# Router decisions worked out in the PSUM bank of the last logits, one bank of logits per head pair, and a slot list cast three units later

## The chip, the cores and the metric

The kernel runs on one core of one Trainium2 chip. Its engines are TensorE (PE, matmuls; PEld is its weight load), VectorE (DVE), ScalarE (ACT), GpSimd (POOL) and SyncE (SP, which issues most of the DMAs). Each takes its instructions from a queue of its own, in order, and waits at an instruction until the semaphores it needs are set. The metric is the device time of one execution in microseconds (us).

## What is computed

Clustered attention feeds a routed mixture of experts.

```python
# attention: q, k, v of (4, 8, 768, 64), centroids (8, 16, 64)
q_assign = argmax(einsum('bhsd,hcd->bhsc', q_n, c_n)); k_assign = ...   # normalized
mask = q_assign[:, :, :, None] == k_assign[:, :, None, :]
scores = where(mask, scale * q @ k.T, -1e9)
x = softmax(scores) @ v             # -> (3072, 512): 4 batches x 768 tokens, 8 heads x 64

# router: 4 groups x 4 experts, F = 1024
g_logits = x @ w_group              # top group, its softmax weight g_w
e_logits = xg @ w_expert[g]         # top expert in the group, its weight e_w
h = maximum(xg[mask_e] @ w1[g, e], 0.0)
out[tok] = (g_w * e_w)[:, None] * (h @ w2[g, e])
```

Both softmax weights come down to 1/sum(exp(l - max l)), since the chosen logit is the greatest.

## The kernel before

**Attention.** There are 32 heads (4 batches of 8). The work of a head is cut into 9 units, 288 in all; in the loop over units, TensorE does for each one `fine` (4 matmuls of scores into a psf bank, L346 and L347), one pass of coarse scores for a later head (psc, L304, from which VectorE takes row maxima, L307) and the product with V of an earlier unit (`av`, 16 matmuls, L372 and L373, into pso). ScalarE takes the exponential (L351, p), GpSimd its low half (L353, pl). Numbers are kept in pairs of fp16 or bf16 (a high and a low half) so that matmuls are fast and nearly exact.

**Beside the units.** Everything else of the attention phase is dealt out between units: normalizing and assigning the next heads (L201 and others), row maxima of a head turned by a transpose (L328, with the copy mr L331, which goes by DMA into a row of A that `fine` needs), and the router. Steps that need a bank of the pool psm (2 banks) give `yield PSM, delay, priority` and are queued in `turns`; `beside` lets one of them in per unit (`GAP` = 1). A plain `yield` waits one unit. The program written in this way is then ordered per engine by a scheduler with a time model of its own, so that an instruction may stand a little before or after where it was written.

**The router, per batch.** `finish` writes a head's result as two halves into the tile xs. After the last head of a batch `store` sends xs to xbuf in HBM, whose rows are the tokens. After every second head `logits` transposes the pair's 128 columns (L596), copies them (L599, xTr), multiplies by the router's weights (L604) and adds the result to lg in SBUF (L610), twice, for token tiles 0 to 2 and 3 to 5. After a batch's last pair `decide` works on 30 groups of 4 logits for each of 128 partitions (6 token tiles x 5 groups): the maximum (rmx L628), the first place that has it (req L630 and L631, rmw L633, roh L635), exp of the differences and its sums (L638 to L641), the one-hot expert of each token (roe L643), the weight (L645 to L650, pay). Rank matmuls over roe (L655 to L659) give each token its place among those of its expert; L662 to L667 make the row number rdi, and six scatters on GpSimd (L678) write token number and weight into the table in HBM.

**The first expert, beside the last batch.** After the third batch `first` picks the expert with most tokens (L803 to L809, f0i), loads its weights (st, L760) and splits them (L780 to L788). Once the third batch's scatters are out it loads that expert's slots from the table (tabA, L836), waits `FIRST + 1` units, casts the slot list (idA, L842) and gathers those rows of xbuf (L916). Its first products are done on TensorE beside the last batch's decision (psh, L954).

**After the last batch** a sorted list of experts is made, the table is read back (tb, L1103), a small matmul by a permutation (L1133) picks slot lists, and then the remaining experts run, each with loads (st), splits (L767, L770), gathers and products (L954, L976, L990).

## Time and profile before

| | us |
|---|---|
| time, median of 3 runs (lowest, highest) | 770.17 (769.25, 773.49) |
| the profiled execution | 771.85 |
| its span | 770.0 |
| TensorE busy | 728.0 (95% of the span) |
| VectorE, GpSimd, ScalarE busy | 604.4, 493.2, 465.8 |

The profiled execution is 1.85 us longer than its span (what lies around it), and 1.68 us above the median. Busy time is the sum over an engine's instructions, without waits. A wait is charged to the engine that stood idle and to the instruction that released it.

### The profile page before, as it was taken

Reading aid. Unit: us, or ns where it says so; the run is one execution under the profiler, and the core shown is the slowest. Engines: PE = TensorE matmul, PEld = TensorE weight load, DVE = VectorE, ACT = ScalarE, POOL = GpSimd, SP = SyncE. Lnnn points to the kernel's source line nnn. Section 1 sums busy time; section 2 is a strip of 40 time slices with the busy share of each in tenths; the row PEclk is TensorE's granted clock in tenths of the full one; section 3 lists DMA queues with packets and bytes.
Section 4 is the critical chain, followed back from the end, with each engine's and each line's share of the span. In section 5 each row is a group of like instructions: output and inputs, shape, how many; then the busy total and the mean of one; then the engine's idle time right before and its main releaser. Section 6 shows DMA issues by size and latency. Waiting matters only on the chain. (4 is left out here: it accounts for less than half of the span.)

```text
span 770.0 us, 26718 instructions
## 1 busy us (share of the span) xinstructions
PE 728.0 (95%) x11086; PEld 625.0 (81%) x11086; DVE 604.4 (78%) x1209; ACT 465.8 (60%) x910; POOL 493.2 (64%) x522
## 2 busy tenths in 40 slices
PE   5899999999999999997999889999999999999996
PEld 3677788878888788886878666788779999999996
DVE  5998978899788998988875545867598898888861
ACT  4567877768777687675886236435444455555542
POOL 9568687779977799776982433425545455654432
PEclk7799999999999999999999999999999999999998
DMA  8857534435345452223321397866778788888821
GB/s 247 198 149 176 147 90 119 156 95 148 88 118 159 95 149 59 68 95 111 84 57 49 65 316 252 261 201 211 228 245 249 236 270 267 260 279 278 267 74 49
DMA packets 80392, 128.28 MB, mean 167 GB/s; under 512 B 8851, under 2 KB 47251, under 8 KB 80264
## 3 DMA queue, kind: packets, MB, share of 16 engines
q1 hardware_dynamic: 74492, 113.12, 50.0%
q0 software_dynamic: 5616, 13.35, 5.1%
q8 instruction: 88, 1.44, 0.9%
q14 instruction: 40, 0.33, 0.1%
q10 hardware_dynamic: 156, 0.03, 0.0%
HBM read 93.20 MB, written 14.11 MB: 139 GB/s over the span
## 5 line engine op out<-in xcount | busy, mean ns | idle before, releaser
L353 POOL TENSOR_TENSOR pl<-p 128x512 f16<-128x512 f32 x278 | 286.8, 1050 | 81.6 <-ACT p L351 77.0
L307 DVE TENSOR_REDUCE mpart<-psc 128x1 f32<-128x512 f32 (+1 forms) x282 | 189.6, 682 | 32.8 <-PE psc L304 32.8
L351 ACT ACTIVATE p<-psf 128x512 f32<-128x512 f32 x288 | 168.5, 595 | 53.2 <-PE psf L347 46.1
L372 PE MATMUL pso<-V,p 128*128 128x65 f16 x1152 | 161.6, 193 | 0.0
L372 PE MATMUL pso<-V,pl 128*128 128x65 f16 x1152 | 161.2, 194 | 0.0
L373 PE MATMUL pso<-V,pl 128*128 128x64 f16 x1152 | 161.0, 191 | 0.0
L373 PE MATMUL pso<-V,p 128*128 128x64 f16 x1152 | 160.9, 191 | 0.0
L346 PE MATMUL psf<-A 82*128 82x384 f16 (+2 forms) x576 | 143.3, 274 | 4.8 <-ACT p L351 3.1
L347 PE MATMUL psf<-B 128*128 128x384 f16 (+2 forms) x576 | 143.6, 274 | 0.0
L373 PEld LDWEIGHTS <-p 128*128 128x128 bf16 x1152 | 112.6, 98 | 21.3 <-issue 0.2
L372 PEld LDWEIGHTS <-p 128*128 128x128 bf16 x1152 | 112.1, 97 | 9.2 <-issue 1.4
L373 PEld LDWEIGHTS <-pl 128*128 128x128 f16 x1152 | 112.8, 98 | 0.7 <-issue 0.4
L304 PE MATMUL psc<-A 80*128 80x512 f16 (+1 forms) x376 | 108.8, 331 | 4.3 <-DVE mpart L307 3.3
L372 PEld LDWEIGHTS <-pl 128*128 128x128 f16 x1152 | 111.2, 97 | 0.3
L957 DVE SCALAR_TENSOR_TENSOR hl<-psh,hh 128x160 f16<-128x160 f32 (+14 forms) x136 | 50.1, 370 | 66.9 <-ACT hh L956 55.7
L956 ACT ACTIVATE hh<-psh 128x160 f16<-128x160 f32 (+14 forms) x136 | 46.1, 346 | 66.8 <-PE psh L954 64.1
L954 PE MATMUL psh<-xT,wh0a 128*128 128x288 f16 (+7 forms) x512 | 74.7, 255 | 0.0
L916 POOL DMA_INDIRECT xg<-xbuf,ri x32 | 41.4, 1294 | 42.4 <-PE psm L926 21.1
L347 PEld LDWEIGHTS <-B 128*128 128x128 f16 x576 | 56.6, 98 | 14.3 <-issue 5.6
L954 PE MATMUL psh<-xT,wh0b 128*128 128x272 f16 (+6 forms) x448 | 65.2, 254 | 2.1 <-DVE xT L928 1.1
L954 PE MATMUL psh<-xT,wl0a 128*128 128x288 f16 (+7 forms) x256 | 64.0, 255 | 0.0
L346 PEld LDWEIGHTS <-A 82*128 82x128 f16 x576 | 55.5, 98 | 10.3 <-DMA A<-mr 1.0
(311 smaller groups left out, 1744.7 us busy)
## 6 DMA issues: line engine op xcount, KB each, us to landing
st<-w SPq DMA_DIRECT2D x128, 512.0 KB
B<-parts SPq DMA_DIRECT2D x64, 192.0 KB
kx<-kT SPq DMA_DIRECT2D x16, 384.0 KB
qx<-qT SPq DMA_DIRECT2D x16, 384.0 KB
vx<-vr SPq DMA_DIRECT2D x16, 384.0 KB
A<-parts SPq DMA_DIRECT2D x32, 192.0 KB
xbuf<-xs SPq DMA_DIRECT2D x4, 1536.0 KB
A<-mk SPq DMA_DIRECT2D x56, 24.0 KB
```

What stands on the lines that cost most here:

```text
L304: last["mm"] = nc.tensor.matmul(out=pc[:, off:off + k1 - k0], lhsT=QA[h % 8][0:80, c * P:(c + 1) * P], rhs=KA[h % 8][0:80, k0:k1], start=T ...
L307: nc.vector.tensor_reduce(out=(mp[:, 0, 0:1], mp[:, :, 1], mp[:, 1, 0:1])[i], in_=pc.rearrange("p (a x) -> p a x", a=n), axis=AX.X, op=ALU ...
L346: nc.tensor.matmul(out=o, lhsT=KA[h % 8][0:82, ks], rhs=QA[h % 8][0:82, q0:q1], start=True, stop=False)
L347: nc.tensor.matmul(out=o, lhsT=KBs[h][:, ks], rhs=QBs[h][:, q0:q1], start=False, stop=True)
L351: cfg["exp"] = nc.scalar.activation(out=p32, in_=pf, func=AF.Exp, scale=QK / (SQ * SQ))
L353: lo = (nc.vector if u in (EARLY if h < 2 else DVE_LO[h % 8] if h < NH - 2 else DVE_END) else nc.gpsimd).tensor_tensor(out=pl, in0=p32, in ...
L372: nc.tensor.matmul(out=O[:, col:col + 65], lhsT=p[:, bs], rhs=vh, start=c == 0 and q == 0 and i == 0, stop=False, skip_group_check=True)
L373: nc.tensor.matmul(out=O[:, col:col + 64], lhsT=p[:, bs], rhs=vl, start=False, stop=c == NCH - 1 and i == 1, skip_group_check=True)
L916: self.got = nc.gpsimd.indirect_dma_start(out=xg[0:n].rearrange("p a d -> p (a d)"), out_offset=None, in_offset=bass.IndirectOffsetOnAxis( ...
L954: self.mm = nc.tensor.matmul(out=ph[:, 0:M], lhsT=w[:, k, fs], rhs=xT[:, a, k], start=i == 0, stop=i == 3 * KD - 1)
L956: nc.scalar.activation(out=hh[:, f], in_=ph[:, 0:M], func=AF.Relu)
L957: self.ev = nc.vector.scalar_tensor_tensor(out=hl[:, f], in0=ph[:, 0:M], scalar=0.0, in1=hh[:, f], op0=ALU.max, op1=ALU.subtract)
```

## The change

The tile xs gets the head pair as its outermost axis, so that a pair is one contiguous block; each pair is stored to xbuf as soon as it is there (16 stores of 384 KB instead of 4 of 1536 KB, in pieces of 512 bytes instead of 2 KB). `logits` does both transposes first, then 18 matmuls into one psm bank and one add of 120 elements per partition instead of two of 60: three turns per pair instead of four. The last pair's sum stays in its PSUM bank, and `decide` works in four stretches of that bank: the logits, req, roh and rdf of before. Its values are fp32 now instead of fp16. The one-hot roe is made before the exponential's branch, for which one copy is added (rog: the group one-hot in SBUF). The bank is held until the weighted sum rss. The first plain `yield` of `decide` moves behind rss, and `first` waits `FIRST + 4` units for the cast.

```diff
-            if hh == H - 1:
-                R.store(b, XSt[b])
             if hh % 2 == 1:
+                R.store(b, XSt[b], hh // 2)
                 gens = [R.logits(b, XSt[b], hh // 2, [(ps_m, "psm"), (ps_f, "psf")] if last else None)]
...
-        for i in range(2):
+        xT = self.sm.tile([P, T, 2, P], F16, name="xTr")
+        banks = banks or [(self.psm, "psm")] * 2
+        for i, (pool, nm) in enumerate(banks):
             yield PSM, 0, 1
...
-            xT = self.sm.tile([P, n, 2, P], F16, name="xTr", bufs=2)
-            self.last["a"] = nc.scalar.copy(out=xT, in_=tp)
-            yield PSM, 1, 1
-            lp = pool.tile([P, 512], F32, name=nm)[:, 0:n * 20].rearrange("p (c x) -> p c x", x=20)
...
+            self.last["a"] = nc.scalar.copy(out=xT[:, n * i:n * i + n], in_=tp)
+        yield PSM, 1, 1
+        bank = self.psm.tile([P, 512], F32, name="psm")
+        lp = bank[:, 0:T * 20].rearrange("p (c x) -> p c x", x=20)
...
+        else:
+            nc.vector.tensor_tensor(out=lp, in0=lp, in1=lg, op=ALU.add)
+            self.lg[b] = bank
...
-        lv = lg.rearrange("p t (g x) -> p (t g) x", x=4)
+        lv, eq, oh, df = (self.lg[b][:, n * G * 4:(n + 1) * G * 4].rearrange("p (g x) -> p g x", x=4) for n in range(4))
...
+        nc.vector.tensor_tensor(out=oh, in0=eq, in1=mw.broadcast_to([P, G, 4]), op=ALU.is_equal)
+        oh = oh.rearrange("p (t g) x -> p t g x", g=5)
+        oe = sm.tile([P, T, 4, 4], F16, name="roe")
+        og = sm.tile([P, T, 4], F32, name="rog")
+        nc.vector.tensor_copy(out=og, in_=oh[:, :, 0])
+        nc.vector.tensor_tensor(out=oe, in0=oh[:, :, 1:5], in1=og.broadcast_to([P, T, 4, 4]), op=ALU.mult)
         nc.vector.tensor_tensor(out=df, in0=lv, in1=mx.broadcast_to([P, G, 4]), op=ALU.subtract)
...
         nc.vector.tensor_tensor(out=ss, in0=se[:, :, 1:5], in1=oh[:, :, 0], op=ALU.mult)
+        yield
...
-        for _ in range(FIRST + 1):
+        for _ in range(FIRST + 4):
             yield
```

On VectorE, from the add of the first batch's last logits to its one-hot experts (before: lg and req, roh, rmw, rmx; L307 are row maxima of the units between):

```order
L610 TENSOR_TENSOR lg<-psm,lg 128x60
L628 TENSOR_REDUCE rmx<-lg 128x30
L630 TENSOR_TENSOR req<-lg,rmx 128x120
L307 TENSOR_REDUCE mpart_198<-psc 128x2
L631 TENSOR_TENSOR req<-req,desc_502 128x120
L638 TENSOR_TENSOR rdf<-lg,rmx 128x120
L633 TENSOR_REDUCE rmw<-req 128x30
L635 TENSOR_TENSOR roh<-req,rmw 128x120
L307 TENSOR_REDUCE mpart_198<-psc 128x1
L641 TENSOR_REDUCE rse<-rdf 128x30
L643 TENSOR_TENSOR roe<-roh 128x96
```

and with the change (psm is the bank that holds all four stretches):

```order
L612 TENSOR_TENSOR psm<-psm,lg 128x120
L630 TENSOR_REDUCE rmx<-psm 128x30
L307 TENSOR_REDUCE mpart_200<-psc 128x1
L631 TENSOR_TENSOR psm<-psm,rmx 128x120
L313 TENSOR_REDUCE m_3880<-mpart_200 128x6
L632 TENSOR_TENSOR psm<-psm,desc_502 128x120
L307 TENSOR_REDUCE mpart_198<-psc 128x1
L634 TENSOR_REDUCE rmw<-psm 128x30
L635 TENSOR_TENSOR psm<-psm,rmw 128x120
L307 TENSOR_REDUCE mpart_198<-psc 128x2
L639 COPY rog<-psm 128x24
L640 TENSOR_TENSOR roe<-psm,rog 128x96
```

The exponential's two steps (L638 and L641 of before) have gone behind roe; one L307 and an L313 more, and the copy rog, stand before it.

On TensorE the rank matmuls of the same batch stood at the end of an `av` (before):

```order
L372 MATMUL pso<-V_173,pl 128x65
L373 LDWEIGHTS pl
L373 MATMUL pso<-V_173,pl 128x64
L655 LDWEIGHTS low
L655 MATMUL psm<-roe,low 128x96
```

and stand now after its first matmul, behind the `fine` and the psc of that unit:

```order
L347 MATMUL psf<-B 128x384
L304 LDWEIGHTS A_169
L304 MATMUL psc<-A_169 128x512
L372 LDWEIGHTS p_3734
L372 MATMUL pso<-V_173,p_3734 128x65
L657 LDWEIGHTS low
L657 MATMUL psm<-roe,low 128x96
```

Three units of TensorE lie between the last logits and the rank in both, and one `fine` and one psc more with the change.

On VectorE, after the last batch's rank matmuls, the row numbers (rdi) came after the weights (pay) before; with the change the weights (L644 to L652) are last, between the first comparisons of the slot list (st, L1100):

```order
L664 TENSOR_TENSOR rps<-psm,cb 128x96
L665 TENSOR_TENSOR rps<-rps,roe 128x96
L644 TENSOR_REDUCE rse<-psm 128x30
L667 TENSOR_REDUCE rds<-rps 128x6
L646 TENSOR_TENSOR rss<-rse,psm 128x24
L669 CAST rdi<-rds 128x6
L670 TENSOR_TENSOR cb<-psm,cb 128x16
L649 TENSOR_REDUCE res<-rss 128x6
L1100 TENSOR_SCALAR st<-sl,rds 128x128
L650 TENSOR_SCALAR res<-res 128x6
L1060 TENSOR_TENSOR c_11365<-cb,ebase 128x16
L1100 TENSOR_SCALAR st<-sl,rds 128x128
```

Four rows behind this piece, with one more comparison (L1100) among them, stands L652, which writes pay; the scatters need both pay and rdi. TensorE's up-projection matmuls (L954 before) between the last logits and the last rank are 20 before and 27 with the change. From L1133 on, TensorE, VectorE, ScalarE and GpSimd have the same instructions in the same order in both.

## Rows read from the trace of the kernel before

**Rows 1.** Busy time by stretch: the stretch (us), its length, then for each engine the busy us and, in brackets, the instructions; at the end TensorE's granted clock as a share of full speed, the DMA engines' busy share and GB/s.

```profile
100.00:200.00 100.00, 98.03 (x1909) 82.06 (x1906) 86.69 (x193) 75.47 (x148) 81.90 (x80) 1.00 0.43 118
300.00:400.00 100.00, 93.94 (x1804) 78.39 (x1802) 85.03 (x193) 72.40 (x141) 81.66 (x81) 1.00 0.30 87
490.00:600.00 110.00, 110.00 (x994) 91.60 (x992) 84.46 (x127) 49.99 (x94) 51.36 (x44) 1.00 0.75 238
452.00:455.00 3.00, 3.00 (x14) 1.93 (x13) 2.06 (x2) 0.29 (x1) 2.50 (x2) 0.50 0.99 313
```

**Rows 2.** Waits between 20 and 425 us, by the engine and line that waited and by the engine and line waited for: us in total, times, longest us.

```profile
PE psm L655 <- DVE roe L643: 4.1, 3, 1.4
...
PE psc L304 <- DVE mpart L307: 3.3, 7, 0.8
...
PE psf L346 <- ACT p L351: 3.1, 5, 1.5
...
DVE idA L842 <- DMA tabA<-table: 1.9, 2, 1.2
...
ACT wh L780 <- DMA st<-w: 1.5, 1, 1.5
```

**Rows 3.** TensorE (PE) in order of time, at places between 152 and 393 us: start us, us, engine, line, operation, out<-in, count, and in square brackets the idle time just before it with what ended that.

```profile
152.20 0.37 PE L604 MATMUL psm<-WR,xTr 128*128 128x20 f16 x9
152.42 0.27 PE L346 MATMUL psf<-A 82*128 82x256 f16 x1
...
153.09 0.19 PE L372 MATMUL pso<-V,p 128*128 128x65 f16 x1
...
153.58 0.22 PE L346 MATMUL psf<-A 82*128 82x128 f16 x1
...
157.46 0.20 PE L655 MATMUL psm<-roe,low 128*128 128x96 f16 x1 [1.36 <-DVE roe L643]
...
164.47 0.38 PE L304 MATMUL psc<-A 80*128 80x512 f16 x1 [0.19 <-DVE mpart L307]
...
260.29 0.38 PE L304 MATMUL psc<-A 80*128 80x512 f16 x1 [0.20 <-DVE mpart L307]
...
354.13 0.27 PE L304 MATMUL psc<-A 80*128 80x256 f16 x1 [0.74 <-DVE mpart L307]
...
358.47 0.27 PE L304 MATMUL psc<-A 80*128 80x256 f16 x1 [0.69 <-DVE mpart L307]
...
392.57 0.33 PE L596 MATMUL psm<-ident,xs 128*128 128x128 f16 x3 [0.91 <-DVE lg L610]
```

**Rows 4.** VectorE (DVE) in order of time around the decision of the first batch, 152 to 159 us; same columns.

```profile
152.61 0.22 DVE L610 TENSOR_TENSOR lg<-psm,lg 128x60 f32<-128x60 f32 x1
152.86 0.28 DVE L628 TENSOR_REDUCE rmx<-lg 128x30 f32<-128x120 f32 x1
153.18 0.86 DVE L630 TENSOR_TENSOR req<-lg,rmx 128x120 f16<-128x120 f32 x1
153.95 0.68 DVE L307 TENSOR_REDUCE mpart<-psc 128x2 f32<-128x512 f32 x1
...
155.43 0.82 DVE L635 TENSOR_TENSOR roh<-req,rmw 128x120 f16<-128x120 f16 x1
...
156.95 0.45 DVE L643 TENSOR_TENSOR roe<-roh 128x96 f16<-128x96 f16 x1
```

**Rows 5.** All instructions of a line, four lines on VectorE: count, shortest/median/longest ns, first and last start, shapes.

```profile
L630 DVE TENSOR_TENSOR req<-lg,rmx x4: 284/854/856, 153.2 to 423.7; 128x120 f16<-128x120 f32 x4
...
L631 DVE TENSOR_TENSOR req<-req,desc x4: 216/450/452, 154.6 to 424.1; 128x120 f16<-128x120 f16 x4
...
L662 DVE TENSOR_TENSOR rps<-psm,cb x4: 249/250/251, 158.5 to 426.2; 128x96 f32<-128x96 f32 x4
...
L201 DVE TENSOR_TENSOR parts<-psm,parts x48: 540/548/559, 62.6 to 321.6; 128x384 f16<-128x384 f32 x48
```

**Rows 6.** VectorE around the decision of the last batch, 423 to 427.3 us, in order of time.

```profile
423.13 0.21 DVE L610 TENSOR_TENSOR lg<-psf,lg 128x60 f32<-128x60 f32 x1
...
425.04 0.26 DVE L643 TENSOR_TENSOR roe<-roh 128x96 f16<-128x96 f16 x1
...
426.16 0.25 DVE L662 TENSOR_TENSOR rps<-psm,cb 128x96 f32<-128x96 f32 x1
...
427.06 0.17 DVE L667 CAST rdi<-rds 128x6 int32<-128x6 f32 x1
```

**Rows 7.** TensorE in the same stretch.

```profile
422.36 0.38 PE L604 MATMUL psf<-WR,xTr 128*128 128x20 f16 x9
422.59 0.28 PE L954 MATMUL psh<-xTA,wl 128*128 128x288 f16 x1
...
424.99 0.29 PE L954 MATMUL psh<-xTA,wh 128*128 128x288 f16 x1
425.35 0.20 PE L655 MATMUL psm<-roe,low 128*128 128x96 f16 x1
```

**Rows 8.** GpSimd (POOL) in order of time, its first scatter of the last batch, and under it two pieces of the chain that ended last (start us, us, what).

```profile
427.51 1.02 POOL L678 DMA_INDIRECT table<-pay,rdi  x1 [9.34 <-DVE st L1098]
...
434.10 8.07 DMA table<-pay,rdi
...
449.49 1.58 PE psm L1133 x12
```

73 lines of the change are left out of this document (32 added, 41 removed).

## Prediction

> **What bounds the kernel now.** I read the stretches first, then the waits, then TensorE, VectorE and GpSimd in order of time where a router step stands. In the attention phase TensorE is busy 98.03 of 100 us, and in the expert phase for every one of 110 us; the third batch's stretch, in which the first expert is prepared, has 93.94 of 100 [rows 1]. So the end is set by TensorE nearly everywhere, and an edit counts for the time that TensorE stands idle because of it, plus what it adds to the one stretch after the last batch in which TensorE has too little to do. In the waits the reader is to see how little the router holds TensorE up: 4.1 us in three waits of the rank matmul for roe, 3.3 us in seven waits of psc for VectorE's row maxima, 3.1 us in five for p [rows 2].
>
> The three rank waits are 1.36, 1.36 and 1.35 us, one per batch but the last (4.1 in all, 1.4 the longest, with the first one shown) [rows 2, 3]. VectorE causes them: from the add of the last logits at 152.61 to the end of roe at 156.95 + 0.45 = 157.40 are 4.79 us, and TensorE starts the rank at 157.46 [rows 3, 4]. Two of the steps in it are the dear ones, req (0.86) and roh (0.82) [rows 4]. The last batch's req takes 0.284 where the others take 0.854, at the same shape [rows 5]; there GpSimd has nothing to do (9.34 us idle up to its first scatter) [rows 8]. Steps that read PSUM show no such spread: 0.249 to 0.251 over four times, 0.540 to 0.559 over 48 [rows 5].
>
> The last batch has another path. Add at 423.13, roe at 425.04, rank 425.35, rps 426.16, rdi 427.06, first scatter 427.51 [rows 6 to 8]. The six scatters, the transfer of the last (8.07 us from 434.10) and the reading back follow one after the other to the matmul at 449.49 [rows 8], where the expert phase begins and from where TensorE is full. What the first scatter is late, the end is late.
>
> **The change, part by part.**
>
> *Decision in PSUM, three batches.* Price of a step of 120 elements on PSUM in fp32: 0.250 for 96 and 0.548 for 384 elements [rows 5] give (0.548 - 0.250) / 288 = 1.03 ns an element, so 0.275 for 120. Below it cannot be much under the 0.250 row; above, 0.548 is the end, if the fixed part counts for more. I take 0.275, from the nearest row, and 0.32 from start to start in a dependent chain, as 152.86 to 153.18 is for a 0.28 step [rows 4]. The stretch from the add to roe has eight router steps: six of 0.32 (1.92), rog of 24 elements at 0.20 (an estimate, between nothing and the 0.32) and roe itself, 0.28. Between them stand three L307, each 0.61 of VectorE's queue (an estimate: the 0.68 of the row at 153.95 less the overlap with the next, by which req's 0.86 takes 0.77 to that row), 1.83, and an L313 of 0.10 (an estimate, half of rog's): 4.33 us instead of 4.79. So the chain itself is only 0.46 shorter, since one L307 and rog come into it. The larger gain is in TensorE's order. A unit is 153.58 - 152.42 = 1.16 us [rows 3], and the rank stands a `fine` and a psc later, 153.09 - 152.42 = 0.67 [rows 3] (bounds: nothing, if that work was ahead of the rank's place in time anyway, and 0.67). New wait: 1.36 - 0.46 - 0.67 = 0.23; with an L307 that itself comes up to 0.2 late for its psc I take 0.40. Gain 0.95 per batch, 2.9 for three. Bounds: 4.1 (no wait left) and, at 0.548 a step, a loss (rival C). The psc waits of 0.19 and 0.20 after the first two batches [rows 3] are VectorE's arrears of the same work; they go: 0.4.
>
> Here the Trainium skill bears on both sides. The trace shows 0.854 against 0.284 for the same step of two SBUF operands, with and without GpSimd at work [rows 5, 8]. "SBUF — State Buffer", section "Who interferes with whom", says that a VectorE instruction with two SBUF inputs contends with a GpSimd instruction that reads SBUF, and that the one that comes second is blocked; by it all steps moved to PSUM are freed, and the trace agrees. Against the change stands "VectorE: DVE Perf Modes", section "Rules for kernel authors": with PSUM sources accept the slow mode, or copy to SBUF first where many operations follow. By that rule alone the step req x desc (0.216 in the clear, 0.450 beside GpSimd [rows 5]) would be better off in SBUF by 0.06 in the last batch and worse by 0.18 in the others; no term of the sum depends on it.
>
> *The bank that is held.* psm has two banks, and `decide` now holds one until rss. The rank takes the other; the next transpose of row maxima (L328, one unit behind the rank on TensorE) takes the held one. It arrives after the rank (at least the 0.20 of its first row), the rest of an `av` (153.58 - 153.09 = 0.49) and a `fine` and psc (0.67) [rows 3]: some 1.4 us behind the rank's start. rss needs by then the subtraction (0.32), the exponential on ScalarE (0.25 to 0.86, the ends of [rows 5], for no row here shows one), and the sum, rps and rss (0.8), with an L307 (0.61) beside the exponential: 1.7 to 2.0 behind roe, and the rank starts when roe ends. So up to 0.6 a batch, and nothing where the exponential runs beside L307 and TensorE itself comes late to L328 (it has just waited for roe); I take 0.13 a batch, near the lower end, 0.4 in all, with 1.8 as the other end.
>
> *Third batch.* Its waits of 0.74 and 0.69 for psc, 1.5 for st and 0.91 behind the cast idA [rows 2, 3] come from the first expert's own steps. The routing is done earlier, f0i and the splits move with it, and so does the last scatter; the cast, written three units later behind it, stands 16 units behind that scatter in both orders (counted by L353 on GpSimd and L307 on VectorE). I leave them as they are: 0, with 2.5 (all VectorE's share gone) and -1 as ends.
>
> *Stores, layout, logits.* Twelve more store DMAs go through SP's queue, between loads that are due much later; DMA engines are busy 0.43 and 0.30 of those stretches [rows 1]. Transposes and matmuls are as many as before. Each pair saves one VectorE add; VectorE has idle time there (86.69 of 100 busy [rows 1]). 0; if the cover were gone, a store of 384 KB in front of a load would cost 1.4 us once (118 GB/s at a busy share of 0.43 is 274 GB/s [rows 1]), less than the one of 1536 KB.
>
> *The last batch.* Both halves' transposes first, so the 18 matmuls stand together: the second half's 9 take 422.59 - 422.36 = 0.23 [rows 7], and all 18 end at 422.36 + 0.46 = 422.82. Then 27 up-projection matmuls instead of 20, each (424.99 - 422.59) / 19 = 0.126 [rows 7]: 3.41, so TensorE reaches the rank at 426.23. VectorE, with the add at 423.2, six steps of 0.32, rog, roe and an hl between them (0.4, an estimate between the 0.25 and 0.55 of [rows 5]), has roe at 426.0: covered. The rank is 0.88 later than 425.35 [rows 7]. rps follows by 0.81 as before (425.35 to 426.16) [rows 6, 7]: 427.04. From rps to pay are now 15 steps in two interleaved chains. In the same kind of interleaving rps to rdi took 427.06 - 426.16 = 0.90 for seven steps [rows 6], 0.13 a step and more where a step depends on the one before; I take 0.14 x 15 = 2.1, so pay starts at 429.14, and the scatter 0.45 after it (427.06 to 427.51) [rows 6, 8], at 429.6: 2.1 later. Bounds: 0.9 (only the rank counts, if pay were in time) and 3.2. I take 2.0. GpSimd's scatters are a chain, so all of it reaches the end. From L1133 on the order is the same, a plain shift.
>
> *Sum:* -2.9 - 0.4 + 0.4 + 0 + 2.0 = -0.9 us on the profiled 771.85, 770.95; on the median of 770.17 it is 769.3. I give the time in terms of the median.
>
> **Rivals.**
>
> A, *the attention gain is larger*. VectorE's freed time also takes the psc waits of the third batch (0.74 + 0.69), the wait of 0.91 and that for st (TensorE's share 1.5) [rows 2, 3], and the rank waits go whole (4.1): -4.1 - 0.4 - 3.8 + 2.0 = -6.3, 763.9. For it: each of these ends at VectorE. Against: L804 and L812's kind of step stays in SBUF, and GpSimd stays full there (81.66 of 100 [rows 1]). 0.20.
>
> B, *gain and loss cancel through the bank*: L328 waits 0.5 to 0.8 for rss in each batch, which gives back 2 us instead of 0.4: 770.9. For it: the pool has two banks only. Against: rss stands 0.3 to 0.6 us behind L328's arrival only if everything falls together. 0.16.
>
> C, *slower: a PSUM step costs its fixed 0.55*. Place: the eight steps before roe. Price: 0.23 a step x 8 = 1.8; the rank waits become 0.4 + 1.8 = 2.2 instead of 1.36, +2.5 for three, and the last batch has 1.6 more ahead of its rank and 1 behind: +2.5 + 0.4 + 2.0 + 2.6 = +7.5, 777.7. It decides from about 0.30 a step on, where the 0.9 of the sum is used up. Against it: the 0.250 row of 96 elements [rows 5]. 0.07.
>
> E, *slower: the last batch alone*. pay comes 1 us later than summed (each of its steps waits for the one before and the slot list's steps stand between), and TensorE's longer idle time before 449.49 prolongs the stretch at half clock (0.50 from 452 to 455 [rows 1]) by as much as 1.5 us: 771.8. Against: TensorE's order to there is filled with the first expert's products. 0.11.
>
> D, *the change doesn't do what it says*: the cast still waits for tabA as before (two waits, 1.9 us [rows 2]). It is part of my sum; that it does go gives 0.9 us less, 768.4.
>
> **How the numbers follow.** Forecast 0.46, A 0.20, B 0.16, C 0.07, E 0.11; D changes the size of the forecast and has no chance of its own. The forecast's own range is 767.5 to 771.5. To hold 8 in 10 it goes down most of the way to A, 764.8, and up past B and E, 773.2. A measurement of this kernel tells apart about 0.5%, 3.85 us: faster than 766.3 is A's greater part, 0.18; slower than 774.0 is C and a part of E, 0.11; between, 0.71.
>
> **What would show it.** Rank waits for roe under 0.6 us each, with the comparison steps at 0.26 to 0.30 in all four batches; L328 with a wait for rss of at most 0.5; the cast idA still waiting over 1 us for tabA; the last batch's first scatter 2 us after 427.51 in its own time, with pay the later of its two inputs; TensorE full from L1133 on. Wrong: PSUM steps over 0.35, rank waits of 1 us or more, or psc waits that are gone in the third batch.

## The result, and the profile of the changed kernel

The changed kernel takes 774.55 us (median of 16 runs, 771.88 to 779.86) where the kernel before takes 770.37 on the same chip (16 runs, 767.31 to 773.49). The ratio is 1.0072, with an interval of 1.0057 to 1.0088: slower by 0.7%. The forecast of 769.3 had the wrong sign, and the time lies above the range's upper end of 773.2. The profiled execution of the changed kernel takes 778.18 us, with a span of 776.1, and lies 3.6 above its median; that of the kernel before takes 771.85, with a span of 770.0, and lies 1.5 above. So the profiles are read for where time goes, and the ratios for how much.

First two of the stretches of [rows 1] in the changed kernel, and three shorter ones: two around the first expert's preparation and one ahead of the expert phase.

```profile
100.00:200.00 100.00, 99.24 (x1936) 83.33 (x1933) 86.36 (x192) 76.20 (x150) 82.87 (x82) 1.00 0.43 118
300.00:400.00 100.00, 91.28 (x1674) 75.27 (x1673) 79.07 (x182) 66.24 (x128) 76.49 (x76) 0.95 0.32 85
...
345.00:360.00 15.00, 10.19 (x187) 8.10 (x184) 10.30 (x34) 5.13 (x11) 8.21 (x8) 1.00 0.44 103
360.00:368.00 8.00, 6.91 (x75) 5.25 (x75) 4.93 (x10) 5.64 (x13) 5.83 (x6) 0.57 0.53 191
...
456.00:460.00 4.00, 1.79 (x9) 1.79 (x9) 1.96 (x4) 2.56 (x5) 0.00 (x0) 0.50 0.90 311
```

Two of the kernel before, for the places that have no row ahead of the prediction:

```profile
345.00:360.00 15.00, 12.16 (x220) 9.65 (x217) 14.58 (x42) 6.24 (x14) 10.35 (x11) 1.00 0.09 24
360.00:368.00 8.00, 6.46 (x120) 5.37 (x118) 5.37 (x11) 6.22 (x11) 5.81 (x7) 1.00 0.84 286
```

In the first batch's stretch TensorE is busy 99.24 us instead of 98.03, so the gain there is real. In 300 to 400 us it is busy 2.7 us less than before, and part of that stretch runs at half clock (0.95 granted on the mean, 0.57 from 360 to 368). From 345 to 360 TensorE has 10.19 busy us where it had 12.16, and from 360 to 368 it does 75 matmuls in the time in which it did 120. The loss is here, and in a second place ahead of 458 us: from 456 to 460 TensorE does 9 matmuls, at half clock.

The waits between 20 and 425 us, as in [rows 2], then TensorE's longest wait between 425 and 480 us:

```profile
PE psf L346 <- ACT p L351: 7.6, 4, 5.1
PE psc L304 <- DVE mpart L307: 4.0, 5, 2.1
...
ACT wh L782 <- DMA st<-w: 5.3, 1, 5.3
...
DVE idA L844 <- DMA tabA<-table: 4.0, 3, 3.5
...
PE psm L1135 <- DVE xT L1118: 7.9, 1, 7.9
```

The three rank waits for roe (4.1 us in [rows 2]) are gone. In their place stands one wait of 5.1 us for p, one of 2.1 for psc and, behind the last batch, one of 7.9 for the first gathered rows (xT), which was 1.6 before.

To see where the lag arises I took the start of each of the attention's 288 exponentials (L351), less the start of the same one in the profile of the kernel before. Over the first 36 units the profiles differ by up to 2.2 us, by when the first loads land (1.51 in the changed kernel's); that part isn't read, and each column is set to zero there. Negative is ahead of the kernel before. The runs named are those of the next section.

| unit | before again (c2) | changed | changed again (c1) | changed again (c3) | first two batches only (e8) | the same again (e14) | third only (e12) | last only (e11) | all but third (e9) |
|---|---|---|---|---|---|---|---|---|---|
| 144 | -0.05 | -1.46 | -0.86 | -1.98 | -1.02 | -1.83 | 0.84 | 0.37 | -1.45 |
| 168 | -0.05 | -2.73 | -2.13 | -3.25 | -2.29 | -3.10 | 0.84 | 0.38 | -2.72 |
| 228 | -0.05 | -2.51 | -1.52 | -2.93 | -2.22 | -3.58 | 1.30 | 0.38 | -2.69 |
| 240 | -0.04 | -4.36 | -3.38 | -4.79 | -2.22 | -3.57 | -0.55 | 0.38 | -2.69 |
| 252 | -0.15 | 1.55 | 1.94 | 0.41 | -2.20 | -3.52 | 3.91 | 1.61 | -1.64 |
| 276 | -0.03 | 4.56 | 4.46 | 2.90 | -2.09 | -3.61 | 2.84 | 3.27 | -0.65 |
| 288 | -0.04 | 4.01 | 3.91 | 2.36 | -2.10 | -3.61 | 2.84 | 2.47 | -1.04 |

The changed kernel gains 2.7 us in two batches and 1.9 more at the third one's rank (units 228 to 240), then loses 5.9 in the twelve units to 252 and 3.0 more to 276. The kernel before, profiled again, runs within 0.2 us of itself, and the changed kernel's two other profiles have the same steps (5.3 and 5.2 us lost in units 240 to 252, 2.5 and 2.5 to 276). Single columns are less sure than that: e11 and e12, whose first two batches are those of the kernel before, differ from it by up to 0.8 us at unit 168, and e12 by 1.3 at 228, so steps under about 1 us aren't read.

*Decision, first batch.* VectorE from the add of the last logits, the comparison and roe, TensorE at the rank, and all four comparisons:

```profile
152.18 0.29 DVE L612 TENSOR_TENSOR psm<-psm,lg 128x120 f32<-128x120 f32 x1 [0.23 <-PE psm L604]
...
153.46 0.28 DVE L631 TENSOR_TENSOR psm<-psm,rmx 128x120 f32<-128x120 f32 x1
...
155.98 0.26 DVE L640 TENSOR_TENSOR roe<-psm,rog 128x96 f16<-128x96 f32 x1
...
156.29 0.20 PE L657 MATMUL psm<-roe,low 128*128 128x96 f16 x1
...
L631 DVE TENSOR_TENSOR psm<-psm,rmx x4: 280/281/291, 153.5 to 429.1; 128x120 f32<-128x120 f32 x4
```

Against [rows 3 to 5]: the comparison takes 0.28 instead of 0.85 in the batches with GpSimd at work, and 0.28 to 0.29 in all four; from the add to the end of roe are 4.06 us instead of 4.79, and the rank has no idle time before it.

*First expert's preparation.* SyncE's queue, ScalarE at the first weights and TensorE behind it, in the changed kernel:

```profile
352.22 0.41 SPq L762 DMA_DIRECT2D st<-w  x1
353.39 0.36 SPq L576 DMA_DIRECT2D xbuf<-xs  x1
353.95 2.01 SPq L762 DMA_DIRECT2D st<-w  x3
...
358.98 1.06 ACT L782 ACTIVATE wh<-st 128x1024 f16<-128x1024 f32 x1 [5.34 <-DMA st<-w]
...
361.09 0.27 PE L346 MATMUL psf<-A 82*128 82x128 f16 x1 [5.06 <-ACT p L351]
```

and in the kernel before:

```profile
357.53 2.13 SPq L760 DMA_DIRECT2D st<-w  x4
...
361.34 1.06 ACT L780 ACTIVATE wh<-st 128x1024 f16<-128x1024 f32 x1 [1.50 <-DMA st<-w]
```

The weights are asked for 5.3 us earlier, but land only 2.4 us earlier: 6.8 us after the first issue (352.22 to 358.98) instead of 3.8. The store of the last batch's first pair now stands between the first and the second load. Just ahead of the cast the transfers are slow; the changed kernel, then the kernel before:

```profile
357.00:359.00 2.00, 0.00 (x0) 0.00 (x0) 0.00 (x0) 0.02 (x1) 0.00 (x0) 1.00 0.99 112
```

```profile
359.00:361.50 2.50, 2.44 (x47) 1.83 (x44) 1.51 (x3) 1.00 (x3) 2.03 (x2) 1.00 0.97 349
```

The DMA engines are busy in both, 0.99 and 0.97, but move 112 GB/s instead of 349. ScalarE, in whose order the cast of these weights comes ahead of the next exponentials, comes to it 6.2 us earlier (358.98 - 5.34 = 353.64 against 361.34 - 1.50 = 359.84) and waits 5.34 for them, and TensorE waits for p behind it.

*Slot list.* The cast that was written three units later still waits; the DMA that brings its rows was issued late. The changed kernel's cast and its SyncE issues (shortest, median, longest ns), then the issues of the kernel before:

```profile
392.58 0.15 DVE L844 CAST idA<-tabA 128x1 int32<-128x1 f32 x1 [3.48 <-DMA tabA<-table]
...
L838 SPq DMA_DIRECT2D tabA<-table x3: 340/345/2601, 388.6 to 392.0; - x3
```

```profile
L836 SPq DMA_DIRECT2D tabA<-table x3: 346/350/351, 389.4 to 390.5; - x3
```

One of the three issues took 2.60 us instead of 0.35. TensorE's wait behind it is the 2.11 us for psc here:

```profile
394.39 0.58 PE L304 MATMUL psc<-A 80*128 80x512 f16 x1 [2.11 <-DVE mpart L307]
```

*The end of the router.* Add of the last logits, roe and the weights (pay) on VectorE, the first scatter on GpSimd, then the pieces of the chain that ended last and TensorE at its long wait:

```profile
428.43 0.28 DVE L612 TENSOR_TENSOR psm<-psm,lg 128x120 f32<-128x120 f32 x1
...
429.39 0.29 DVE L632 TENSOR_TENSOR psm<-psm,desc 128x120 f32<-128x120 f32 x1
...
430.96 0.26 DVE L640 TENSOR_TENSOR roe<-psm,rog 128x96 f16<-128x96 f32 x1
...
433.92 0.18 DVE L652 RECIPROCAL pay<-res 128x6 f32<-128x6 f32 x1
...
434.39 1.23 POOL L680 DMA_INDIRECT table<-pay,rdi  x1 [10.92 <-DVE st L1100]
...
440.99 9.52 DMA table<-pay,rdi
...
451.22 4.00 DMA st<-w
...
458.21 2.74 PE psm L1135 x12
460.95 5.53 PE psy L978 x24
...
458.21 1.03 PE L1135 MATMUL psm<-perm,tb 16*128 16x16 f32 x4 [7.89 <-DVE xT L1118]
```

The lag at the permutation matmul is 458.21 - 449.49 = 8.72 [rows 8], and it adds up: 5.30 at the add (428.43 against 423.13 [rows 6]; 1.51 of it is the difference of the first loads that the table sets to zero), 1.58 from the add to the first scatter (5.96 against 4.38), 0.01 over the six scatters, 1.45 in the landing of the last (9.52 against 8.07) and 0.38 from there on. TensorE's granted clock is 0.50 for 10.2 us instead of 3.4: from 455.7, while the wait still lasts, to 466.0, so for 7.7 us behind it (451.7 to 455.2 in the kernel before). The lag grows to 10.7: the twelve matmuls and the 24 behind them end at 466.48, against 455.80 before (451.07 + 4.73). Then it falls to 6.0, since the kernel before has six waits of its own between 458 and 489 us, 4.5 us together, where the changed one has two of 0.8 together at the same matmuls. From 500 us on it stays at 6.0 with the same instructions in the same order.

### The profile page after: what moved, and what is told of

Its sections match the earlier page's. It is cut to its first block, busy times and chain, and to the rows that moved or that the text cites. A ratio compares the mean times of both kernels' runs of the same rounds, so it can differ in the third digit from the quotient of the medians.

```text
span 776.1 us, 26736 instructions
## 1 busy us (share of the span) xinstructions
PE 734.1 (95%) x11086; PEld 630.0 (81%) x11086; DVE 600.9 (77%) x1197; ACT 464.7 (60%) x910; POOL 496.5 (64%) x522
## 5 line engine op out<-in xcount | busy, mean ns | idle before, releaser
L307 DVE TENSOR_REDUCE mpart<-psc 128x1 f32<-128x512 f32 (+1 forms) x282 | 190.2, 684 | 32.5 <-PE psc L304 31.9
L351 ACT ACTIVATE p<-psf 128x512 f32<-128x512 f32 x288 | 169.6, 595 | 60.9 <-PE psf L347 55.4
L372 PE MATMUL pso<-V,p 128*128 128x65 f16 x1152 | 164.0, 195 | 0.0
L372 PE MATMUL pso<-V,pl 128*128 128x65 f16 x1152 | 163.2, 195 | 0.0
L373 PE MATMUL pso<-V,pl 128*128 128x64 f16 x1152 | 163.0, 192 | 0.0
L373 PE MATMUL pso<-V,p 128*128 128x64 f16 x1152 | 162.8, 192 | 0.0
L346 PE MATMUL psf<-A 82*128 82x384 f16 (+2 forms) x576 | 145.0, 277 | 8.4 <-ACT p L351 7.6
L347 PE MATMUL psf<-B 128*128 128x384 f16 (+2 forms) x576 | 145.2, 277 | 0.0
L304 PE MATMUL psc<-A 80*128 80x512 f16 (+1 forms) x376 | 110.7, 336 | 5.3 <-DVE mpart L307 4.0
```

Of the source, the lines that this page charges most:

```text
L304: last["mm"] = nc.tensor.matmul(out=pc[:, off:off + k1 - k0], lhsT=QA[h % 8][0:80, c * P:(c + 1) * P], rhs=KA[h % 8][0:80, k0:k1], start=T ...
L307: nc.vector.tensor_reduce(out=(mp[:, 0, 0:1], mp[:, :, 1], mp[:, 1, 0:1])[i], in_=pc.rearrange("p (a x) -> p a x", a=n), axis=AX.X, op=ALU ...
L346: nc.tensor.matmul(out=o, lhsT=KA[h % 8][0:82, ks], rhs=QA[h % 8][0:82, q0:q1], start=True, stop=False)
L347: nc.tensor.matmul(out=o, lhsT=KBs[h][:, ks], rhs=QBs[h][:, q0:q1], start=False, stop=True)
L351: cfg["exp"] = nc.scalar.activation(out=p32, in_=pf, func=AF.Exp, scale=QK / (SQ * SQ))
L372: nc.tensor.matmul(out=O[:, col:col + 65], lhsT=p[:, bs], rhs=vh, start=c == 0 and q == 0 and i == 0, stop=False, skip_group_check=True)
```

## The experiments

All ratios are to the kernel before, run beside it on the same chip. Its median goes from 766.95 to 772.73 from one such series to another, so ratios are compared and not times. Three theories go through them. "Position" (P where an expectation gives letters) says that the first expert's preparation is now two units too early against the loads; "tail" (T) that the weights (pay), now last, hold the scatters; "stores" (U) that the pair stores stretch loads and the reading back.

**Stores of a batch issued together at its end** (e1).

```diff
-                R.store(b, XSt[b], hh // 2)
+                if hh == H - 1:
+                    for k in range(H // 2):
+                        R.store(b, XSt[b], k)
```

> The changed kernel with one edit: the four stores of a batch are issued together after its last pair, as before. Theory S (the store of the fourth batch's first pair stands on SP's queue and on the DMA engines beside the first expert's weight loads, whose first one so lands 6.8 us after its issue instead of 3.8): the wait of ScalarE for the first weights falls from 5.3 to about 1.5 us, TensorE's wait for p from 5.1 to about 1.5, and the time falls by 2 to 4 us against the changed kernel, to 770.5 to 772.5. Rival O (the weights are late because the routing itself and its queue order moved): the wait stays near 5 and the time near 774.5.

Ratio 1.0091 (1.0055 to 1.0126). The wait for the first weights falls from 5.3 to 3.3 us, and the one long issue of the slot list stays (2598 ns):

```profile
ACT wh L784 <- DMA st<-w: 3.3, 1, 3.3
```

So the store between the loads is about 2 us of that wait (in the changed kernel's three profiles it is 4.5 to 5.8), but not all of it, and the time is no better.

**The cast one unit behind instead of four** (e2).

```diff
-        for _ in range(FIRST + 4):
+        for _ in range(FIRST + 1):
```

> The changed kernel with FIRST + 1 units before the cast instead of FIRST + 4. If the three units do what they are for: VectorE's wait for the slot list grows from 4.0 us by 2 to 3.5, TensorE's by as much, the time to 775 to 778. If the order puts the cast by other rules, the wait stays at 4.0 and the time at 774.5. If the wait of 3.5 us in the one profile came from that execution alone (a load of the list whose issue took 2.6 us instead of 0.35), a profile here shows the issue at 0.35 and the wait shorter than in the changed kernel, even with the earlier cast.

Ratio 1.015 (1.0118 to 1.0182), the slowest of all. Of the three alternatives the second holds for the wait, but not for the time. The cast waits 3.7 us in all, hardly less than the 4.0 at +4: its place in VectorE's order is the same, and only the steps behind it moved up. The three units seem worth having, in this kernel 0.3 to 0.8% (1.015 against 1.0072 to 1.0116; against the last of these alone the intervals overlap), but they don't do what they say to the cast.

**The kernel before with the new layout and pair stores, nothing else** (e3).

```diff
-            if hh == H - 1:
-                R.store(b, XSt[b])
             if hh % 2 == 1:
+                R.store(b, XSt[b], hh // 2)
```

> The kernel before with one edit: the tile in pair order and a store for every pair; logits, decision and cast as before. Theory S: nothing changes in the first three batches' rank waits (4.1 us in all), ScalarE's wait for the first weights grows from 1.5 to 4 us or more, and the time grows by 2 to 4 us over the kernel before, to 772.5 to 774.5. Rival O: no change, 770.4 within 1.

Ratio 1.0035 (1.0007 to 1.0064). The wait for the first weights is the old one, although a store comes shortly ahead of the loads:

```profile
354.65 0.37 SPq L576 DMA_DIRECT2D xbuf<-xs  x1
357.62 2.11 SPq L759 DMA_DIRECT2D st<-w  x4
...
ACT wh L779 <- DMA st<-w: 1.6, 1, 1.6
```

The stores cost something by themselves, about 2.7 us (0.5 to 4.9), and not at the first weights. In its profile the permutation matmul comes 3.3 us later than in the kernel before's: 0.3 at the last scatter, 1.4 in that scatter's landing (9.51 instead of 8.07) and 1.6 in the weights behind it (5.24 instead of 3.63).

**The last batch's weights first** (e4): the subtraction and exponential right behind the maximum.

```diff
         nc.vector.tensor_reduce(out=mx, in_=lv, axis=AX.X, op=ALU.max)
+        if early:
+            nc.vector.tensor_tensor(out=df, in0=lv, in1=mx.broadcast_to([P, G, 4]), op=ALU.subtract)
+            nc.scalar.activation(out=df, in_=df, func=AF.Exp, scale=1.0 / (XS * WRS))
```

> The changed kernel with one edit: for the last batch alone the difference and the exponential come right behind the maximum, as before. Theory T (the weights pay hold up the first scatter): from the add of the last logits to the first scatter 5.2 us instead of 6.0, pay done before rdi, and everything up to the permutation matmul 0.8 earlier; the end gains 0 to 0.8, since the first weights of the expert phase are partly waited for after that. Rival: the rank is later by the two steps now ahead of it and the scatter is no earlier. The attention phase is the changed kernel's instruction for instruction, so this profile also shows whether the waits of 5.1 and 2.1 us on TensorE there come again.

Ratio 1.0123 (1.0088 to 1.0158). From the add (428.88) to the first scatter (435.05) are 6.17 us instead of 5.96: roe came later by as much as pay was to come earlier.

```profile
428.88 0.28 DVE L612 TENSOR_TENSOR psm<-psm,lg 128x120 f32<-128x120 f32 x1
...
432.28 0.26 DVE L643 TENSOR_TENSOR roe<-psm,rog 128x96 f16<-128x96 f32 x1
...
435.05 1.03 POOL L684 DMA_INDIRECT table<-pay,rdi  x1 [11.14 <-DVE st L1104]
```

"Tail" falls in this form: pay's place alone doesn't set the scatter. That the number of steps in the one chain does is argued, not shown.

**The changed kernel again** (c1).

> The changed kernel itself once more, as a control on the same chip as the next three. What its profile shows again is the kernel's, what it doesn't was one execution's: TensorE's waits of 5.1 us (for p, behind the first weights) and 2.1 us (for psc, behind the slot list) and the 29.8 us from the add of the last logits to the permutation matmul (26.5 before). 774.5 to 779.

Ratio 1.0116 (1.0083 to 1.0148); 5.8 us of wait for the first weights, 2863 ns for the longest slot-list issue, 7.0 before the permutation matmul. The picture repeats, in c3 too (4.5, 2430 ns and 7.3 us).

**Third batch's last logits two units later** (e5), so that the first expert's preparation stands where it stood.

```diff
+        if k == self.KD - 1 and b == self.B - 2:
+            yield
+            yield
         yield PSM, 1, 1
```

> The changed kernel with one edit: the third batch's last logits (and with them its decision, the first expert's choice and its weight loads) come two units later, where they stood before. Theory P (the change moved these steps two units ahead, where the first weight load meets the pair's store and the slot list's load meets a load of program code): TensorE's 5.1 and 2.1 us fall to 1.5 and 1, the rank waits stay away, and the attention phase ends 8 to 9 us earlier than in the changed kernel, 3 us earlier than before; the time falls by 6 to 9 us against the control. Rival Q (what costs is the held bank and the new order on VectorE, wherever it stands): waits as in the control, time within 2 us of it.

Ratio 1.0108 (1.0078 to 1.0139), against 1.0116 for the changed kernel on the same chip. The wait for the first weights falls to 2.5 us, and the slot list's issues take 0.35 again, but TensorE waits elsewhere:

```profile
353.24 0.38 PE L304 MATMUL psc<-A 80*128 80x256 f16 x2 [2.20 <-DVE mpart L307]
...
366.00 0.49 PE L596 MATMUL psm<-ident,xs 128*128 128x128 f16 x6 [2.85 <-DVE wl L793]
```

By the lag table's measure it ends 2.0 us behind instead of 3.9, and the time is the same. "Position" alone falls: two units shift the loss from one wait to two others. The first weights, with no store near, still land only 6.1 us after their first issue.

**The same, and the last batch decided by the old steps in SBUF** (e6).

```diff
+        elif b == self.B - 1:
+            nc.vector.tensor_tensor(out=lg, in0=lp, in1=lg, op=ALU.add)
         else:
             nc.vector.tensor_tensor(out=lp, in0=lp, in1=lg, op=ALU.add)
```

> As the run before, and the last batch decided in SBUF by the old steps. Theory T2 (decision in PSUM costs in the last batch, where GpSimd is idle and the SBUF steps are short): add of the last logits to first scatter 4.4 to 4.8 us instead of 6.0, 1.3 less at the end. Rival: the two banks of logits joined and the 27 matmuls ahead of the rank hold it up alike, 5.5 or more.

Ratio 1.0059 (1.0036 to 1.0083). The first scatter starts 4.83 us after the add, as 428.73 and 433.56 show, against 5.96 in PSUM.

```profile
428.73 0.27 DVE L617 TENSOR_TENSOR lg<-psm,lg 128x120 f32<-128x120 f32 x1
...
433.56 1.02 POOL L708 DMA_INDIRECT table<-pay,rdi  x1 [9.85 <-DVE st L1128]
```

Nearly half of what e5 is slower comes from the last batch's new decision: 1.1 us at the scatter, about 3.8 us (0.5%) in the time, where 1.3 was expected; the two intervals leave 0.8 to 6.7 us.

**The same, with the old layout and stores** (e7): e6 with the two edits of e3 undone.

> As the run before, with the old layout and one store of 1536 KB per batch. If the pair stores with their pieces of 512 bytes cost by themselves (the kernel before with pair stores was 0.35% slower), 1 to 3 us less than the run before, and under the kernel before by 3 to 5: 766 to 768. If they cost only where the first weight load meets one, no difference to the run before.

Ratio 1.0043 (1.0023 to 1.0063), not distinguishable from e6, and not the 3 to 5 us under the kernel before that were expected.

For the rest the kernel before was given both versions of logits and decision, and a condition says which batch takes the new one:

```diff
     def logits(self, b, xs, k, banks=None):
+        return (self.logits_new if b < self.B - 2 else self.logits_old)(b, xs, k, banks)
```

The decision takes the PSUM steps where the logits lie in a bank. Layout and stores are the old ones where nothing else is said.

**The first two batches alone** (e8), and again on another chip (e14).

> The kernel before with the new logits and the decision in PSUM for the first two batches alone; the third and fourth batch, the stores, the layout and the cast as before. Theory P2 (the change gains in the batches beside which nothing else stands, and loses where its earlier steps meet the first expert's preparation, and in the tail): two rank waits of 1.36 gone, -2.5 us of lag by the end of the second batch's decision, kept to the end: 767 to 768.5, below both kernels. Rival R (time saved on TensorE there is given back later, as waits for GpSimd or the loads): lag 0 by the end of the attention phase, 770.4.

> The version with the new logits and decision in the first two batches alone once more, to see whether its small gain (0.9976, interval 0.9953 to 0.9999) holds on another chip. Theory: lag -1.5 to -2.6 by the end of the attention phase, ratio 0.996 to 0.999. Rival (chance): ratio 1.000 or above, lag within 0.5.

Ratios 0.9976 (0.9953 to 0.9999) and 0.9966 (0.9949 to 0.9983): faster than both kernels. ScalarE's wait for the first weights and TensorE's before the permutation matmul are of the old size in e8 (1.5 and 1.4; the second is 4.9 in e14), and the third batch keeps its rank wait:

```profile
PE psm L715 <- DVE roe L682: 1.3, 1, 1.3
...
PE psm L1193 <- DVE xT L1176: 1.4, 1, 1.4
```

**All but the third batch** (e9), condition `b != self.B - 2`, in the changed kernel.

> The changed kernel with the third batch's logits and decision as before (pair stores, FIRST + 4, and the fourth batch as changed). Theory P2: the lag that the changed kernel picks up between units 240 and 276 (6.0 to 8.0 us in its two profiles) falls to under 2, TensorE's wait behind the first weights is 1.6 us again; the tail stays 3 us longer; 772 to 774. Rival (the loss there comes from the fourth batch's own joined logits): lag there still 5 or more, 777 to 779.

Ratio 1.0076 (1.0047 to 1.0106). Attention ends 1.0 us ahead in the lag table, and units 240 to 252 lose 1.1 us instead of 5.9, so most of that loss is the third batch's; but before the permutation matmul TensorE waits 7.5 us, and the time is as bad as the whole change's.

**The changed kernel with the old layout and stores** (e10): the two edits of e3 undone.

> The changed kernel with the old layout and one store of 2-KB pieces per batch; everything else as changed. Theory U (the pair stores cost twice: beside the first weight load, and in the time from the last scatter to the first weights, which is 13.4 to 14.8 us in all profiles with them and 11.7 and 12.1 in the two without): the wait for the first weights 3 to 3.5 us instead of 5.3 to 5.8, the stretch from the last scatter to the first weights 12, time 2 to 4 us under the changed kernel. Rival: stretch 13.4 or more, time as the changed kernel's.

Ratio 1.0089 (1.0057 to 1.012). The wait for the first weights is 3.5, as in e1, the longest slot-list issue 2847 ns. Without the pair stores the change is no faster, and the time from the last scatter to the first weights, expected at 12 us, is 13.9 (7.68 for the landing and 6.17 for the weights).

**The kernel before again** (c2), one execution.

> The kernel before once more, as a control for its profile: waits of TensorE for roe 4.1 us, for p behind the first weights 1.5, no half clock in the attention phase after 40 us, the stretch from the last scatter's issue to the first weights 11.7 us, all within 0.3 us if they are the kernel's; 769 to 772.

774.0 us, span 772.3; every wait that is read here is that of [rows 2] within 0.3 us. Its slot-list issues take 0.35.

**The last batch alone** (e11), condition `b == self.B - 1`.

> The kernel before with the new logits and decision in the last batch alone; stores, layout and cast as before. Theory T3 (the later first scatter is not passed on one to one: TensorE, with seven more up-projections ahead of the rank, is done with the first expert's products earlier and stands idle in one piece before the permutation matmul, and after such a piece the clock is halved for 10 us instead of 3.4): attention as before, scatter 1.6 later, wait before the permutation matmul 5 us or more instead of 1.6 to 1.8, half clock of 10.2 us, time +3.5 to +6 on the kernel before. Rival (plain shift): +1.6 to +2, wait under 3 us, half clock 3.4 us.

Ratio 1.008 (1.0052 to 1.0108). This one part costs as much as the whole change.

```profile
432.29 1.23 POOL L738 DMA_INDIRECT table<-pay,rdi  x1 [10.92 <-DVE st L1158]
...
PE psm L1193 <- DVE xT L1176: 6.5, 1, 6.5
...
PE psc L304 <- DVE idA L902: 1.8, 1, 1.8
```

The first scatter comes 5.96 us after the add at 426.33, as in the changed kernel. The wait before the permutation matmul is 6.5 us instead of 1.6, with 10.2 us at half clock, 6.4 of them behind it, and 2.1 us are lost in units 240 to 288 already (0.38 to 2.47 in the table), one wait of 1.8 behind the cast idA among them. Of the part's edits only the joined logits stand in those units; how they lead to that wait wasn't followed.

**The third batch alone** (e12), condition `b == self.B - 2`, the cast at `FIRST + 4`, so that this edit is in the run too.

> The kernel before with the new logits and decision in the third batch alone, and FIRST + 4; stores and layout as before. Theory P2 (its steps meet the first expert's preparation): one rank wait less (-1.4), then TensorE waits 3 to 3.5 us behind the first weights and 2 behind the slot list, half clock after them: lag +3 to +4 by unit 276, tail as before, time +2 to +4. Rival (the loss needs the other parts, the store or the fourth batch's joined logits): lag within 1, time within 1.5 of before.

Ratio 1.005 (1.003 to 1.007). Its wait for the first weights is 3.4 us with no store near, TensorE's longest for p 3.2, and 6.8 us at half clock follow as in the changed kernel (0.57 granted over 360 to 368). The wait behind the slot list, expected at 2 us, isn't there:

```profile
ACT wh L840 <- DMA st<-w: 3.4, 1, 3.4
...
360.00:368.00 8.00, 6.07 (x58) 4.48 (x58) 4.15 (x7) 6.31 (x12) 5.11 (x5) 0.57 0.59 185
```

**The first two batches, with layout and pair stores** (e13).

> The version with the new logits and decision in the first two batches alone, and pair stores in the new layout. Theory (pair stores cost in the tail, where the stretch from the last scatter's issue to the first weights was 14.8 us with them in the kernel before, and 11.7 and 12.1 without): stretch 13.4 or more, wait before the permutation matmul 4 us or more, time 2.5 to 3.5 above the version with old stores. Rival (that stretch varies by itself): 12 here, no difference.

Ratio 1.0004 (0.9986 to 1.0022), against 0.9976 and 0.9966 without them: the pair stores cost 0.3 to 0.4% here, as in e3 (against e8 alone the intervals overlap). Attention is no slower for them (4.0 us ahead at the end), so it isn't there; the wait before the permutation matmul is 4.5 us, but it is 4.9 in e14, which has the old stores and is faster. One place does go with the stores: the last scatter takes 8.2 to 9.6 us to land in nine of the ten profiles that store pair by pair (7.7 in e6), and 6.2 to 8.1 in the nine others, e1 with its stores at the end among them (7.7). That this is where the 0.3% goes isn't shown.

**The changed kernel, beside these** (c3).

> The changed kernel on the same chip, to set the parts against the whole: if the parts add up, its ratio to the kernel before is the sum of the four parts' (first two batches -0.24%, third, last, pair stores +0.35%), 0.7 to 1.2%.

Ratio 1.0076 (1.0049 to 1.0102).

Added up: first two batches -0.3%, third +0.5, last +0.8, pair stores +0.3 to 0.4, in all +1.3 to 1.4%. The whole change measures 0.7 to 1.2%, so the parts seem to overlap; the four intervals combined reach down to about 0.9%. That one delay at the end of the router lies beside another is argued, not shown.

## Why the prediction was wrong, step by step

The sum was -0.9 us, and the change measures +4.2. In time the parts are -1.9 and -2.6 us for the first two batches (e8, e14), about +3.8 for the third (e12) and +6.1 for the last (e11), and +2.7 for the stores (e3). Two steps failed above all: the third batch at 0, and the last batch as a plain shift.

**Rank waits, -2.9: the mechanism right, the size too small.** All three are gone whole, where 0.40 each was to stay: the chain from the add to roe takes 4.06 us and not 4.33. By unit 168 two of them have given 2.7 us; the units of the third batch's rank give 1.9 (228 to 240). e8 and e14 show the gain of two batches in the time, 0.24 and 0.34%. The psc waits after the first two batches, -0.4, can't be told apart within that.

**A PSUM step at 0.275: right**, 0.280 to 0.292 in four batches; rival C falls. The rule of the Trainium skill, "SBUF — State Buffer", section "Who interferes with whom", had VectorE's steps on PSUM freed of GpSimd, and the trace agrees: 281 ns with GpSimd at work, 291 without. Not every step on two SBUF operands was slow beside GpSimd, though: in the kernel before rdf (L638, the shape of req, but fp32) took 0.271 to 0.273 us in the first three batches, with GpSimd at work, and 0.277 in the last. The other, "VectorE: DVE Perf Modes", section "Rules for kernel authors", preferred SBUF where many operations follow; in the last batch, where GpSimd is idle, the trace agrees too: the step with desc takes 0.29 in PSUM against 0.216 in SBUF [rows 5].

**The held bank, +0.4: nothing.** No wait of L328 for rss is in the waits. Rival B falls.

**The third batch, 0: the first step that failed.** "The routing is done earlier, f0i and the splits move with it ... I leave them as they are: 0, with 2.5 ... and -1 as ends." The waits were taken as VectorE's (rival A says that each of them ends there, but the one for st ends at a DMA [rows 2]), and the step that hurt was a DMA and ScalarE: with the decision come the first expert's weight loads, 5.3 us earlier on SyncE, and ScalarE's cast of them, 6.2 us earlier and in order ahead of the exponentials; the loads take 6.8 us instead of 3.8 up to the cast. That costs 5.1 us of TensorE and then 6.8 us at half clock. By the table the changed kernel loses 5.9 us in units 240 to 252, and e12 alone loses 4.5 there. e9, without the third batch's new steps, loses 1.1, hardly more than such columns differ by without cause. e1, e10 and e12 show that about 2 us of the 5.3 are the store between the loads, and the rest comes without one. Why the loads take longer even then isn't shown, but it goes with the third batch's new steps: from the first issue to the cast are 3.7 to 3.9 us in the eight profiles that have its old ones, pair stores or not, and 4.8 to 7.4 in the eleven that have the new ones, 6.1 to 6.7 in e5 to e7 with no store near. One thing changes with them: the batch's first scatter is issued 0.2 us behind the first load in the eight, and none of its packets has moved when the cast starts; in the eleven it is issued 0.4 to 1.3 us ahead of it, and its packets move among the loads'. No run separates that from the rest.

**The slot list: named as unchanged, and it got worse.** The cast's wait of 1.9 became 4.0. It isn't the place of the cast (e2) but the issue of 2.6 us on SyncE, and this stands in each profile that has the changed third batch and the changed last batch together without the two-unit delay (2.4 to 3.0 us in seven profiles), and not in e12 (0.69) or e9, e11 (0.35). In the same stretch one packet of program code (16 KB) is under way. The queue's packets, MB and share of 16 engines, in the changed kernel from 388 to 391.6 us, then in the kernel before from 386.5 to 391.6:

```profile
q8 instruction: 1, 0.02, 5.2%
```

```profile
q8 instruction: 1, 0.02, 1.2%
```

That is 0.052 x 16 x 3.6 = 3.0 us against 0.012 x 16 x 5.1 = 1.0.

The other traces bear this out: in all seven such a packet starts within 0.3 us of the list's first issue, takes 2.7 to 3.2 us, and ends 0.38 us before the long issue does, about the length of a normal issue (0.35); in e12 it overlaps the issue of 0.69; in the other eleven it has ended before the first issue starts. That the code load holds up the issue, and why it takes so long itself, is still argued from the two lying together; no run separates them.

**Stores and layout, 0: failed, by a little.** The bound was 1.4 us once. e3 and e13 measure 0.3 to 0.4%, 2.3 to 3.1 us, with intervals that still hold 1.4. e7 and e10, which take the stores out of a kernel that loses at the third or last batch, gain nothing that can be told.

**The last batch, +2.0: its first half right, "a plain shift" wrong.** Add to scatter is longer by 1.58 (predicted 2.0, with pay the later input, as it is): from rps to pay are 2.13 us, as summed (2.1), and rps stands only 0.33 us further behind the add than before, where 0.81 was summed. But e11 alone costs 0.8%, some 6.1 us. Three things came on top. While attention still runs, units 240 to 288 lose 2.1 us in e11 (0.38 to 2.47) and 1.7 in e9 (-2.69 to -1.04), where I had costed the joined logits at nothing. TensorE, which had 1.6 us to wait before the permutation matmul, waits 6.5 to 8.0. And its clock is then at half for 10.2 us, of which 7.7 lie behind the wait in the changed kernel and 6.4 in e11, instead of 3.4. Rival E had this last mechanism, at 1.5 us for the clock and 771.8 in all; the clock measures 2.0 in the profiled pair (8.27 us for the twelve matmuls and the 24 behind them, instead of 6.31), the later pay that E supposed didn't come, and E had no price for the rest. The longer landing of the last scatter and the weights behind it, which SyncE issues only after it has issued the reading back of the table (9.52 and 4.00 against 8.07 and 3.63), isn't the last batch's: in e11 the landing takes 6.58, and it goes with the stores.

The prediction also took TensorE as full from the permutation matmul on, but it read that from 490 us on [rows 1]; between 458 and 489 the kernel before waits 4.5 us in six waits. So in the profiled pair 4.7 us of the lag come back by 500 us. What is left of the difference between profile and time isn't settled: from the permutation matmul to the end the same instructions take 315.5 to 317.1 us in the four profiles of one chip (c3, e11, e12, e13) and 320.1 to 321.5 in the eight of two others (c1, e1 to e7), whichever kernel it is.

The clock around these waits, by the profiles' granted clock. Before the permutation matmul: a wait of 1.4 us in e8 with no half clock; waits of 1.0 in e7, 1.6 and 1.8 in the kernel before (twice) and 2.6 in e12, each with 3.4 us at half clock; 4.5 in e13, 4.7 in e3 and 4.9 in e14, each with 6.8; 5.9 in e6 to 8.0 in e2, in eleven profiles, each with 10.2. In the eleven the clock falls while the wait still lasts, and 5.5 to 8.1 us of the 10.2 lie behind it. A longer wait there cost its own length and, but for e7 and e8, a longer stretch at 0.50.

## What to carry to other kernels

When a decision is made earlier, list the DMAs that are issued behind it and which in-order engine will stand waiting for them: here ScalarE's wait at the cast of the first weights, passed on to TensorE, cost as much as the three waits that the change removed (e12 loses 4.5 us there, the waits were 4.1). A change that helps in the body of a loop needn't be made in its last turns: the new decision in the first two of four batches is worth 0.3%, in the last two it costs 0.5 and 0.8%. At the end of a phase, cost a delay with the idle time of the engine that waits, and with the slower clock behind it.

## What was not expected of the hardware

A step on PSUM takes the same 0.28 us with GpSimd at work where one on two SBUF operands takes 0.85. A SyncE issue of a small DMA, 0.35 us elsewhere, took 2.4 to 3.0 us once in each of seven profiles, with a code packet of 2.7 to 3.2 us under way in each that ended 0.4 us before it. A stretch at half clock at a long wait of TensorE lasted 3.4, 6.8 or 10.2 us, longer at longer waits, and in the attention the changed kernel has two in its first expert's preparation (360.1 to 366.9 and 394.3 to 397.7, and such two in its other profiles) where the kernel before has none between 43 and 451 us.
